# A state-space scan with a low-rank mixer: seven output blocks turned to token order by VectorE instead of TensorE

## The chip, the cores and the metric

The kernel runs on one core of a Trainium2 chip. The metric is the device time of one execution in microseconds (us), lower is better. Three runs of the kernel before took 227.44, 227.70 and 227.95 us; the median is 227.7 us.

Five engines work side by side, each on its own queue of instructions and in the order of that queue: TensorE (PE in the profile; PEld is its weight load), VectorE (DVE), ScalarE (ACT), GpSimd (POOL) and SyncE (SP, which here does nothing but issue DMA transfers). They wait for one another by semaphores.

## The reference

Two stages. The first is a gated linear recurrence over 768 tokens for 4 batches and 8 heads (head width 32, state width 16), worked in chunks. The second takes the heads side by side as 256 channels `x` (4, 768, 256) and computes

```python
xt = x.transpose(0, 2, 1)
h = xt @ U @ V                       # low rank 32, over the tokens
u = x + h.transpose(0, 2, 1)
ch = np.maximum(u @ w_ch1, 0.0) @ w_ch2   # 256 -> 1024 -> 256
return (u + ch).astype(np.float32)   # (4, 768, 256): tokens are rows
```

All of it is fp32. The weights come as 64-bit floats, which the kernel reads as pairs of 32-bit words and turns into fp32 itself.

## The kernel before

**Layout.** Tokens are handled with channels on the partitions: `yT[b]` is a tile of 128 partitions by 2 halves of channels (n = 0, 1) by 768 tokens. The mixer works on blocks (b, j): batch b, tokens j\*384 to j\*384 + 383, so there are eight blocks, (0,0) to (3,1). A function `block(n, j)` (line 751) gives the 128 x 384 piece of half n.

**Order.** Nothing is scheduled by a planner. The lists of words in `PLANS` (lines 34 to 73) give the order in which the program issues its work, and each engine's queue keeps that order. A word is a letter with numbers. The ones needed below are:

- `p`: product of all tokens with U (line 728), its PSUM result copied by ScalarE to `pT` (line 732)
- `x`: product of `pT` with V (line 739) into four PSUM banks, two tagged "x" and two tagged "z"
- `a`: VectorE adds these four products to `yT` (line 748); this frees the banks
- `S`: the block is split into three fp32r parts "near" (ScalarE, line 769), "far" and "both" (VectorE, lines 756 and 761), as tile `u`
- `f`, `e`, `h`: first and second product with `w_ch1` on TensorE, and the third step, on VectorE, which makes "far" and "both" of the result
- `g` and `m`, `M`: the scan's score products on TensorE (line 528), which take all four "x" and "z" banks, and VectorE's masking of them (line 541)
- `i`, `n`, `j`: the scan's output products (lines 654 and 678). The first product of `j` waits for a VectorE instruction, usually the one-column copy `settled` (line 605), which in turn waits for the products of `i` or `n`
- `d`: the next piece of `down(j)` for a block

**down(j)** (line 849) is a generator: each `d` in the plan runs it to the next `yield`. A block of batches 1 to 3 takes 14 pieces, a block of batch 0 takes 6. The pieces are products with `w_ch2` (line 774); then `whole` (line 857) adds the result to `yT` on VectorE; and the last two pieces, one for each half n, put the block into token order:

- three TensorE transposes of 128 x 128 into a PSUM bank tagged "w" (line 901)
- one ScalarE copy of 128 x 384 from PSUM into the tile `o` (line 902)
- behind the second half, one DMA of the whole block, 384 rows of 1 KB (line 904)

The block (3,1) goes through `rows(j)` (line 819) and not through `down`; so `down` handles seven blocks and its branch for `last` is never entered. Seven blocks with two halves each give 14 places in the queues. They come in seven pairs, and the plan sets what stands around them:

```
PLANS[1] ... R6 d1.0 g4 m4 p0 d1.0 M4 | PLANS[2] x1 R1 n0 s0 a1.0        block (0,0)
PLANS[2] ... e1.0.7 h1.0.6 i0 d2.1 d2.1 j0 h1.0.7 g2 y0 s2 m2 M2 n1 i1 d1.0 S1.1 f1.1.0   block (0,1)
PLANS[3] ... t2 e1.1.6 e1.1.7 p0 d1.0 | PLANS[4] x1 h2.1.6 h2.1.7 d2.0 d2.1 a1.0          block (2,0)
```

The wrapper `Kept` (lines 159 to 175) remembers the last VectorE instruction for the loads that are to start no earlier. It makes line 170 the line of nearly every VectorE instruction in the profile, so those are told apart by their tiles.

## Time and profile before

| what | value |
|---|---|
| median of three runs | 227.7 us |
| span of the profiled execution, first to last instruction | 225.2 us |
| median less span (no view of the profile shows what lies there) | 2.5 us |
| TensorE busy | 217.0 us, 3016 products |
| VectorE busy | 157.3 us, 339 instructions |
| ScalarE busy | 120.8 us, 283 instructions |
| GpSimd busy | 6.2 us |
| line 901, transposes | 42, pairs of places from 74.7 to 212.2 us |
| line 902, copies | 14, 476 to 483 ns each |
| line 904, stores of 384 KB | 7, issued from 78.4 to 213.1 us, 372 to 388 ns of SyncE's queue each, 2.5 to 4.4 us to landing |
| granted TensorE clock | 1.000 over the span |

The profile is of one execution, so durations read from it are summed against its span of 225.2 us; the profile names no other time of its own execution. The median of the separate runs lies 2.5 us above that span. In the timeline each row has the start in us, the time in us that the instructions of the row cover, the engine, the line, the operation, the tiles (written <- read), the shape and the count; in brackets stands how long the engine had been idle before it and what it waited for. Products on TensorE are pipelined: one starts while the one before it is still draining, so the distance from one start to the next tells more than a duration does. The same holds to a smaller degree on VectorE.

### The profile page before, as it was taken

Reading aid. Unit: us, or ns where it says so; the run is one execution under the profiler, and the core shown is the slowest. Engines: PE = TensorE matmul, PEld = TensorE weight load, DVE = VectorE, ACT = ScalarE, POOL = GpSimd, SP = SyncE. Lnnn points to the kernel's source line nnn. Section 1 sums busy time; section 2 is a strip of 40 time slices with the busy share of each in tenths; the row PEclk is TensorE's granted clock in tenths of the full one; section 3 lists DMA queues with packets and bytes.
Section 4 is the critical chain, followed back from the end, with each engine's and each line's share of the span. In section 5 each row is a group of like instructions: output and inputs, shape, how many; then the busy total and the mean of one; then the engine's idle time right before and its main releaser. Section 6 shows DMA issues by size and latency. Waiting matters only on the chain.

```text
span 225.2 us, 6994 instructions
## 1 busy us (share of the span) xinstructions
PE 217.0 (96%) x3016; PEld 180.5 (80%) x3016; DVE 157.3 (70%) x339; ACT 120.8 (54%) x283; POOL 6.2 (3%) x22
## 2 busy tenths in 40 slices
PE   7978899999999999999999999999999999999994
PEld 5657676665666678768999998799998799999993
DVE  3388899897996767879538827978557925765641
ACT  2353765579875425754616615385356434934820
POOL 4022000000000000000000000000000000000000
PEclk9999999999999999999999999999999999999999
DMA  6889779981950023642006200200000100010022
GB/s 89 141 120 147 113 171 220 240 177 41 167 76 4 0 73 41 89 59 73 4 3 90 75 1 3 76 0 0 4 0 3 43 30 0 3 68 3 0 70 70
DMA packets 69294, 14.56 MB, mean 65 GB/s; under 512 B 63568, under 2 KB 67472, under 8 KB 69264
## 3 DMA queue, kind: packets, MB, share of 16 engines
q1 hardware_dynamic: 69264, 14.13, 31.9%
q8 instruction: 23, 0.38, 0.7%
q14 instruction: 7, 0.06, 0.1%
HBM read 10.98 MB, written 3.15 MB: 63 GB/s over the span
## 4 chain that ended last, share of the span: by engine, by line
PE 89%; SPq 5%; DVE 2%; DMA 2%; issue 1%
PE x L774 33%; PE z L774 31%; SPq L196 4%; PE y L678 4%; PE y L654 4%; PE w L728 3%; PE w L901 2%; PE w L699 2%; PE x L528 2%; DMA bc<-in_C_dram 2%; PE w L496 2%; PE w L563 2%; PE x L739 2%; PE z L528 1%; PE z L739 1%
## 5 line engine op out<-in xcount | busy, mean ns | idle before, releaser
L170 DVE SCALAR_TENSOR_TENSOR words<-words 128x768 fp32r<-128x768 f32 (+6 forms) x44 | 34.6, 804 | 2.1 <-ACT words L420 1.1
L774 PE MATMUL z<-u,w 128*128 128x384 f32 x144 | 33.0, 349 | 0.0
L774 PE MATMUL x<-u,w 128*128 128x384 f32 x144 | 32.7, 346 | 0.0
L779 ACT ACTIVATE x<-x 128x384 f32<-128x384 f32 (+1 forms) x31 | 14.6, 470 | 28.2 <-PE x L774 27.6
L774 PEld LDWEIGHTS z<-u,w 128*128 128x128 f32 x144 | 25.0, 188 | 1.4 <-ACT z L779 0.2
L774 PEld LDWEIGHTS x<-u,w 128*128 128x128 f32 x144 | 24.9, 188 | 1.0
L774 PE MATMUL x<-words,w 128*128 128x384 f32 x120 | 24.7, 340 | 0.2 <-DVE yT L170 0.2
L774 PE MATMUL z<-words,w 128*128 128x384 f32 x120 | 24.6, 336 | 0.0
L779 ACT ACTIVATE z<-z 128x384 f32<-128x384 f32 (+1 forms) x30 | 14.2, 473 | 14.7 <-PE z L774 14.1
L170 DVE SCALAR_TENSOR_TENSOR words<-x,words 128x384 fp32r<-128x384 f32 x24 | 13.3, 553 | 11.7 <-ACT words L808 11.7
L774 PEld LDWEIGHTS x<-words,w 128*128 128x128 f32 x120 | 20.8, 188 | 0.5 <-DVE yT L170 0.4
L774 PEld LDWEIGHTS z<-words,w 128*128 128x128 f32 x120 | 21.1, 188 | 0.0
L170 DVE TENSOR_TENSOR yT<-x,yT 128x384 f32<-128x384 f32 x15 | 8.3, 553 | 16.0 <-PE x L774 15.4
L170 DVE SCALAR_TENSOR_TENSOR words<-z,words 128x384 fp32r<-128x384 f32 x24 | 13.2, 551 | 5.0 <-ACT words L808 5.0
L808 ACT ACTIVATE words<-x 128x384 fp32r<-128x384 f32 x24 | 11.8, 492 | 6.5 <-PE x L774 6.5
L808 ACT ACTIVATE words<-z 128x384 fp32r<-128x384 f32 x24 | 11.8, 492 | 4.5 <-PE z L774 4.5
L170 DVE TENSOR_TENSOR yT<-z,yT 128x384 f32<-128x384 f32 x15 | 8.3, 552 | 8.3 <-PE z L774 8.3
L654 PEld LDWEIGHTS y<-T,Sm 32*64 32x64 f32 x352 | 8.6, 131 | 4.7 <-issue 1.4
L654 PE MATMUL y<-T,Sm 32*64 32x64 f32 x352 | 11.9, 238 | 0.5 <-DVE settled L170 0.5
L678 PEld LDWEIGHTS y<-M,x 64*32 64x32 f32 x768 | 8.7, 105 | 4.5 <-issue 2.7
L678 PE MATMUL y<-M,x 64*32 64x64 f32 x768 | 11.3, 224 | 1.0 <-issue 0.7
L170 DVE SCALAR_TENSOR_TENSOR S<-S,kept,w 128x64 f32<-128x64 f32 x40 | 11.2, 279 | 1.6
(139 smaller groups left out, 382.3 us busy)
## 6 DMA issues: line engine op xcount, KB each, us to landing
words<-in_moe_w_ch_dram SPq DMA_DIRECT2D x7, 512.0 KB, 5.4
x<-in_x_dram SPq DMA_DIRECT2D x24, 128.0 KB, 3.5
out_dram<-o SPq DMA_DIRECT2D x5, 384.0 KB, 2.5
bc<-in_B_dram SPq DMA_DIRECT2D x24, 64.0 KB, 3.5
bc<-in_C_dram SPq DMA_DIRECT2D x12, 128.0 KB, 3.1
out_dram<-words SPq DMA_DIRECT2D x2, 384.0 KB, 3.6
words<-in_moe_w_ch_dram SPq DMA_DIRECT2D x2, 256.0 KB, 3.7
out_dram<-o SPq DMA_DIRECT2D x3, 128.0 KB, 1.7
```

What stands on the lines that cost most here:

```text
L170: self.last = call(*args, **kwargs)
L196: op = nc.sync.dma_start(**kwargs)
L496: nc.tensor.transpose(out=tp[:, i, v], in_=s["BC"][:, i, c + v].rearrange("p h n -> p (h n)"), identity=ident)
L528: nc.tensor.matmul(out=g[r][cols, c], lhsT=s["T"][rows, 0, c, cols], rhs=s["Cm"][rows, :, :, ts(2 * c + p, Q)].rearrange("r v t i -> r v i ...
L563: nc.tensor.matmul(out=s["A"][p][ts(r, Q), v], lhsT=s["bd"][half, v, 2 * r:2 * r + 2].rearrange("p h n -> p (h n)"), rhs=x_sb[k][half, v, ...
L654: product = nc.tensor.matmul(out=y[p][ts(r % 2, H), r // 2, c], lhsT=own[ts(r, Q)], rhs=s["T"][ts(r, Q), 1, :, ts(2 * c + p, Q)].rearrange ...
L678: product = nc.tensor.matmul(out=y[p][ts(i, Q), n, c], lhsT=x_sb[k][half, c, h], rhs=s["M"][half, h // 2, c, h % 2], start=fresh(k, p, [i] ...
L728: nc.tensor.matmul(out=p[ts(q, Q)], lhsT=U_sb[:, c], rhs=ytok[b][:, c, ts(q // 2, P)], start=(c == 0), stop=(c == NC - 1), skip_group_chec ...
L739: nc.tensor.matmul(out=h[q][:, :HS], lhsT=pT[rows], rhs=V4[rows], start=True, stop=True, skip_group_check=True)
L774: nc.tensor.matmul(out=t, lhsT=lhsT, rhs=rhs, start=start, stop=True, skip_group_check=True)
L779: nc.scalar.activation(t, t, AF.Copy, scale=1.0 + EPS)
L808: nc.scalar.activation(gs[j, m // 2][0][:, m % 2], t, AF.Relu, scale=NEAR)
```

## The change

In every block but (3,1), that is wherever `down` gets to this point, each half n is turned by one VectorE instruction, a stream transpose of 128 x 384 that transposes each 32 x 32 square in its place, from `yT` straight into the output tile. The squares then hold 32 tokens on 32 partitions by 32 channels. Four DMAs store a half, one for each group g of 32 partitions; each moves 384 pieces of 32 channels, 128 bytes, to its rows in the output. A half no longer uses TensorE, a "w" bank or ScalarE. The number of stores grows from 7 to 56. The transpose is called on the engine itself, not through the wrapper `Kept`, so it doesn't change which instruction the loads wait for.

```diff
@@ def down(j)
             o = (mix.tile([P, 2 * WCOLS], FP32, tag="o", name="o") if b else raw.tile(
                 [P, 2 * WCOLS], FP32, tag="words", name="words", bufs=NWORDS))
+            turned = o[:, :NCB * HS].rearrange("p (n t) -> p n t", n=NCB)
             o = o[:, :HS // P * DM].rearrange("p (k n d) -> p k n d", k=HS // P, n=NCB)
             for n in range(NCB):
...
                 if last and n:
                     yield
                     return
+                if (b, j) != (NB - 1, NBL - 1):
+                    nc.vector.transpose(out=turned[:, n], in_=block(n, j))
+                    for g in range(P // Q):
+                        nc.sync.dma_start(
+                            out=out[b, ts(j, HS)].rearrange(
+                                "(k t) (n g c) -> n g t k c", t=Q, n=NCB, c=Q)[n, g],
+                            in_=turned[ts(g, Q), n].rearrange("p (k c) -> p k c", c=Q))
+                    yield
+                    continue
                 t = bank("w", HS // P, P)
                 for k in range(HS // P):
                     nc.tensor.transpose(out=t[:, k], in_=block(n, j)[:, ts(k, P)], identity=ident)
                 nc.scalar.copy(out=o[:, :, n], in_=t)
```

Here P is 128, Q is 32, HS is 384, NCB is 2, NB is 4 and NBL is 2.

## The prediction

> **What bounds the kernel now.** I read the page first: busy times, slices, chain.

> ```profile
> PE 217.0 (96%) x3016; PEld 180.5 (80%) x3016; DVE 157.3 (70%) x339; ACT 120.8 (54%) x283; POOL 6.2 (3%) x22
> ...
> PE   7978899999999999999999999999999999999994
> ...
> DVE  3388899897996767879538827978557925765641
> ...
> PE 89%; SPq 5%; DVE 2%; DMA 2%; issue 1%
> ```

> TensorE is the bound: busy in every slice, 89% of the chain. VectorE's 70% is uneven: some slices are full, others a quarter. So the price of more VectorE work depends on the place. Line 901 and what a 384-column VectorE instruction costs come from that line's own view and the groups by shape:

> ```profile
> L901 PE MATMUL w<-ident,yT x42: 270/272/329, 74.7 to 212.2; 128*128 128x128 f32 x42
> ```

> ```profile
> L170 DVE TENSOR_TENSOR yT<-x,yT 128x384 f32<-128x384 f32 x15 | 8.3, 553 | 16.0 <-PE x L774 15.4 <-PE z L739 0.4 <-PE x L739 0.2
> ...
> L170 DVE TENSOR_SCALAR words<-words 128x384 int32<-128x384 int32 x2 | 0.6, 353 | 0.0
> ```

> Three transposes move TensorE's last end by 0.33 us (212.11 to 212.44 in the chain), 0.11 each; the 0.27 is mostly pipeline. Between products of another shape a place takes up to 0.48. So 14 x 0.33 = **4.6 us** is the most that TensorE alone can give; the 0.15 us more at six places are filling, which the next product pays instead.

> **What a transpose costs VectorE.** No transpose is in the trace. The nearest row has the same size and type: 553 ns long (425 for 256 columns in the same view, so 1.0 ns a column), but such adds start 0.465 us apart (78.90, 79.36, 79.83, 80.29). Below it, 353 ns for one source at a higher rate, about 0.27 apart by the same overlap. Above it, two passes: the 128x768 rows, 958 ns. I take **T = 0.50 us** of queue: the nearest row plus 0.03, an estimate for the first 32 columns at 1.0 ns, before a square can be given out turned; 0.27 and 0.96 stay for the range. [...]

> VectorE gains 14 x 0.50 = 7.0 us of queue, ScalarE loses 14 x 0.48 = 6.7, neither of which is the sum. What counts is what stands behind each pair in VectorE's queue. I followed the timeline at the seven pairs. Signs are changes of the end time.

> **(0,0), +0.74.**

> ```profile
> 77.27 0.55 PE L901 MATMUL w<-ident,yT 128*128 128x128 f32 x3
> 77.41 0.27 ACT L732 COPY pT<-w 128x128 f32<-128x128 f32 x1 [0.78 <-PE w L728]
> 77.75 0.59 PE L739 MATMUL x<-V,pT 32*128 32x384 f32 x2
> 78.90 0.55 DVE L170 TENSOR_TENSOR yT<-x,yT 128x384 f32<-128x384 f32 x1
> 79.71 0.59 PE L774 MATMUL x<-words,o 128*128 128x384 f32 x1
> ```

> VectorE has no gap from 74.44 to the adds at 78.90, and both transposes come before them. The add frees bank "x" at 79.45; TensorE takes it at 79.71, 0.26 later. With 2T in front it is free 1.00 later: 1.00 - 0.26 = +0.74, whatever TensorE saved (its second set only filled the wait for the pT copy). VectorE's next idle time, 3.10 us before 85.87, ends the delay there.

> **(0,1), +0.77.**

> ```profile
> 100.04 0.55 DVE L170 SCALAR_TENSOR_TENSOR words<-x,words 128x384 fp32r<-128x384 f32 x1
> 100.23 0.88 PE L901 MATMUL w<-ident,yT 128*128 128x128 f32 x6
> 100.51 0.14 DVE L170 COPY settled<-slot 128x1 f32<-128x1 f32 x1
> ...
> 101.04 0.42 PE L654 MATMUL y<-T,Sm 32*64 32x64 f32 x10
> ```

> Both transposes fall between the first two VectorE rows, and `settled` releases j0 on TensorE. It ends at 101.65 instead of 100.65; j0 had 0.39 to spare, so +0.61 where six transposes stood. Then `settled`, the step h, four masks and the split follow with one gap of 0.07: the split's "far" part ends 0.93 later than 104.46, and f1.1.0, which wanted it at 104.62, waits to +0.77.

> **(1,0), -0.66.** At 119.14 the delay goes into 0.42 us that VectorE idles before 120.44, at 124.23 it hits only copies whose user comes 7 us later (L728 at 135.7). TensorE keeps 2 x 0.33.

> **(1,1), -0.10.** VectorE's transposes fit into its idle 1.14 us before 138.63 and 0.60 before 140.91. But TensorE gains little: the masks from 138.63 to 140.05 free the banks of the next score products, which start at 140.05 already, and the next masks, to 142.33, free those of x1, whose last bank starts at 142.38. The transposes filled these waits.

> **(2,0), +0.56.**

> ```profile
> 176.13 0.96 DVE L170 SCALAR_TENSOR_TENSOR words<-words 128x768 fp32r<-128x768 f32 x1
> ...
> 177.53 0.56 DVE L170 TENSOR_TENSOR yT<-x,yT 128x384 f32<-128x384 f32 x1 [0.44 <-PE z L739]
> ...
> 178.14 1.66 PE L774 MATMUL x<-words,w 128*128 128x384 f32 x8 [0.15 <-DVE yT L170]
> ```

> VectorE is full from 170.43 to 177.09, idles 0.44, then does the add for which TensorE waits, with no slack. Both transposes come before it: 1.00 - 0.44. The 0.48 us of line 901 at 176.11 only covered the pT copy.

> **(2,1), -0.22.** At 192.17 the 0.52 us idle before 192.23 hides it and TensorE gains 0.33. At 194.94 the transpose stands before two h steps and the split. "Far" ends at 199.69, for a product that wants it at 200.12: slack 0.43. It moves by -0.33 + 0.50 to 199.86, and TensorE, 0.66 early, waits for it, about 0.44.

> **(3,0), -0.60.** Idle 0.38 before 208.56, 0.41 before 210.99 and 1.16 before 212.71 hide both. TensorE gains 0.66; the last "far" (215.20, wanted at about 215.5) costs some 0.05 back.

> **SyncE and DMA.** 56 stores at 0.38 us of queue are 21 us instead of 2.7, spread over seven blocks; a block's eight take 3 us where SyncE idles for 10 and more. The loads behind them are used many us later, so nothing. Cover gone would mean a load 3 us late. A 128-byte packet took 13 ns in this trace (x loads, reads), a 1 KB packet 47: a block is 3072 x 13 / 16 = 2.5 us of sixteen engines, against 1.1. Writing such rows isn't in the trace. At the end the eight stores of (3,0) are out by about 214.5 and the last three start at 218.9: cover 4 us. [...]

> **Added waits.** A reused output tile waits for eight stores instead of one: a handful of semaphore waits of 17 to 51 ns (rows at lines 902 and 901) in front of a transpose, +0.1 in all at (2,0).

> **Sum:** 0.74 + 0.77 - 0.66 - 0.10 + 0.56 - 0.22 - 0.60 + 0.10 = +0.6. The span goes from 225.2 to 225.8; with the same 2.5 us around it **228.3 us**, +0.3%. What a measurement can tell from no change is about 0.2%, 0.46 us. The sum changes by 7 us for each us of T (twice at three pairs, once at (2,1)), so T from 0.465 to 0.60 gives +0.35 to +1.3: the likeliest case's own range is 227.9 to 229.0.

> **Rivals.**
> 1. *VectorE's delay is hidden and TensorE's time comes back* (not slower). For: the chain, 89% TensorE. Against: the three places above. It decides by T: below 0.41 the sum is negative. At T = 0.27 it is 0.28 + 0.31 - 0.66 - 0.10 + 0.10 - 0.45 - 0.60 = -1.1: 226.6. With all three waits gone it ends at 227.7 - 4.6 = 223.1.
> 2. *Two passes*, T = 0.96: (0,0) 1.66, (0,1) 1.69, (2,0) 1.48, (2,1) about +0.2, the idle times at (1,0) and (3,0) overrun, together -0.5: +4.4, so 232.1. Against: the row of equal columns and bytes is the near one, and nothing in the trace takes two passes for one.
> 3. *Small stores bind*: SyncE or the sixteen engines fall behind and the last stores come 1 to 3 us late, 229.3 to 231.3. It needs over 60 ns per written 128-byte packet (5.9 us x 16 / 1536).
> 4. *The change doesn't do what it says*: the condition holds in all seven blocks, so 42 transposes and 14 copies go; I give it nothing.

> **Chances.** Forecast (227.7 to 229.1) 0.55; rival 1 0.25, of which 0.07 below 226; rival 2 0.10; rival 3 0.10. The forecast's low end is within 0.2%, as is a part of rival 1: same 0.25, faster 0.15, slower 0.60. Range 226.5 to 230.5.

> **What would show it.** In the profile after: 14 VectorE transposes of 0.5 to 0.6 us; TensorE idle, for the first time after 30 us, before L774 near 80, before L654 near 101 and before L774 near 178.6, each released by VectorE; no such wait at (1,0) and (3,0). I am wrong if the transposes take 0.9 us, if those three waits are missing, or if the last store of (3,0) lands after 218.

## The result, and the profile after

The changed kernel takes 229.92 us (median of 13 runs, 228.85 to 231.14) against 228.01 us (13 runs, 227.29 to 229.26) for the kernel before: **1.0082 times the time, interval 1.0057 to 1.0106**, some 1.9 us slower. The forecast was +0.3%, 0.6 us. Here and below the medians are of all executions, while a ratio and its interval leave out those more than 1.5% above the fastest of the same kernel (three in run 4, two in run 10).

The page of the changed kernel: busy times, the granted clock in 40 slices (tenths of full speed), the chain by engine.

```profile
PE 216.5 (95%) x2974; PEld 179.0 (78%) x2974; DVE 163.8 (72%) x353; ACT 115.1 (50%) x269; POOL 6.2 (3%) x22
...
PEclk9985999999999999999999999999999999999999
...
PE 84%; DVE 8%; SPq 3%; issue 2%; DMA 1%; ACT 1%; DVEq 0%
```

42 TensorE products and 14 ScalarE copies are gone, and VectorE has 14 instructions more. ScalarE lost 5.7 us of busy time, VectorE gained 6.5. TensorE lost only 0.5, in a span that is 3 us longer. In the chain TensorE gives up 5 points and VectorE takes 6: the end now hangs on VectorE in places. The profiled span, 228.2 us, belongs to an execution of 229.92 us, so 1.7 us lie around a span, not the 2.5 that the forecast took. The profile of before came from an execution with a short start.

**Where the time came from.** I paired every TensorE product, other than the transposes, of a run with the same product of the profile before. How much later it starts is its shift. The table has the growth of the shift over the stretch in which each block is turned (boundaries, in the time of before: 73.9, 98.0, 112.0, 137.2, 172.0, 188.0, 207.0 and 221.6 us). "Start" is the shift that a run already has at 73.9 us, ahead of anything that the change touches. There the executions of one kernel differ too: the two profiles of the changed kernel by 0.7 us.

| run, us | start | (0,0) | (0,1) | (1,0) | (1,1) | (2,0) | (2,1) | (3,0) | sum after start |
|---|---|---|---|---|---|---|---|---|---|
| forecast | | +.74 | +.77 | −.66 | −.10 | +.56 | −.22 | −.60 | +.5, and .1 for waits |
| changed kernel | 1.0 | +.86 | +.81 | −.39 | +.69 | +.40 | −.15 | −.19 | +2.0 |
| changed, again | 1.7 | +.81 | +.81 | −.39 | +.34 | +.41 | −.16 | −.19 | +1.6 |
| one store a block | .9 | +.86 | +.81 | −.39 | +.03 | +.40 | −.14 | −.19 | +1.4 |
| VectorE turn alone | 2.1 | +.86 | +.96 | −.03 | +.03 | +.40 | +.19 | +.01 | +2.4 |
| no turn | .9 | −.11 | +1.41 | −.39 | +.02 | −.03 | −.52 | +.05 | +.4 |
| no turn, again | .8 | −.11 | −.11 | −.38 | −.04 | −.04 | −.53 | −.18 | −1.4 |
| turn behind the add | 2.1 | +.74 | +.47 | +.69 | +.34 | −.03 | +.62 | −.18 | +2.7 |
| turn placed | .9 | +.13 | +.35 | +.68 | +.21 | −.03 | +.63 | −.19 | +1.8 |
| small stores alone | .9 | −.04 | +.01 | −.04 | −.04 | .00 | .00 | +.01 | −.1 |
| turn where nobody waits | 1.1 | −.05 | +.01 | −.38 | −.05 | −.03 | −.52 | −.18 | −1.2 |
| the same, with (0,1) | 1.3 | −.05 | +2.13 | −.37 | +.78 | −.02 | −.53 | −.19 | +1.7 |
| code pages moved | 9.7 | +.86 | +2.13 | −.39 | +.04 | +.41 | −.15 | +.07 | +3.0 |
| wait filled | 1.0 | +.85 | +.80 | −.38 | +.01 | +.41 | −.14 | −.19 | +1.4 |

**The new instruction.** The view of the changed kernel's line 901 (engine, operation, tiles, count; shortest, middle and longest duration in ns; first and last start):

```profile
L901 DVE STREAM_TRANSPOSE o<-yT x10: 566/570/572, 122.1 to 213.8; 128x384 f32<-128x384 f32 x10
L901 DVE STREAM_TRANSPOSE words<-yT x4: 536/562/571, 77.3 to 102.9; 128x384 f32<-128x384 f32 x4
```

It is one pass: 570 ns beside the add's 553. Two back to back delay what stands behind them by 0.96 us, so T is 0.48; the forecast had 0.50.

**(0,0).** Two rows of before, the masks M of the "z" banks and the first products with V that take those banks:

```profile
76.91 0.74 DVE L170 TENSOR_TENSOR M<-z,causal 128x256 int32<-128x256 int32 x2
77.76 0.59 PE L739 MATMUL z<-V,pT 32*128 32x384 f32 x2
```

The timeline of the changed kernel:

```profile
78.40 0.56 DVE L901 STREAM_TRANSPOSE words<-yT 128x384 f32<-128x384 f32 x1
78.69 0.91 PE L739 MATMUL x<-V,pT 32*128 32x384 f32 x4 [0.39 <-ACT pT L732]
78.88 0.72 DVE L170 TENSOR_TENSOR M<-z,causal 128x256 int32<-128x256 int32 x2
79.32 1.24 PE L739 MATMUL z<-V,pT 32*128 32x384 f32 x4
...
80.83 0.55 DVE L170 TENSOR_TENSOR yT<-x,yT 128x384 f32<-128x384 f32 x1
```

The size is as forecast, the place is not. The second transpose stands before the masks M of the two "z" banks, and the products with V want those banks. They came 0.01 us behind those for the "x" banks before (77.75, 77.76), and come 0.63 behind them now (78.69, 79.32). The wait before line 774 that the forecast named does not appear, since the delay was paid two steps earlier. The 0.39 us before 78.69 is the wait for the pT copy, which the second set of transposes used to fill.

**(0,1).** Two transposes in one row, then `settled`, then the product that waits for it:

```profile
102.39 1.03 DVE L901 STREAM_TRANSPOSE words<-yT 128x384 f32<-128x384 f32 x2
103.34 0.11 DVE L170 COPY settled<-slot 128x1 f32<-128x1 f32 x1
...
103.51 0.41 PE L654 MATMUL y<-T,Sm 32*64 32x64 f32 x9 [1.32 <-DVE settled L170]
```

This is the wait that the forecast named, and the longest that the change makes.

**(2,0).** The transpose, the add behind it, and the product that wants its bank:

```profile
180.48 0.57 DVE L901 STREAM_TRANSPOSE o<-yT 128x384 f32<-128x384 f32 x1
180.97 0.52 DVE L170 TENSOR_TENSOR yT<-x,yT 128x384 f32<-128x384 f32 x1
...
181.55 1.14 PE L774 MATMUL x<-words,w 128*128 128x384 f32 x5 [1.02 <-DVE yT L170]
```

The wait is 0.15 before, 0.48 of transposes that covered another wait, and 0.4 of new delay.

**(1,1).** What happens here was not in the forecast. TensorE stands still twice for no semaphore ("issue"):

```profile
143.56 0.48 PE L654 MATMUL y<-T,Sm 32*64 32x64 f32 x10 [0.36 <-issue]
...
147.84 0.48 PE L654 MATMUL y<-T,Sm 32*64 32x64 f32 x10 [0.41 <-issue]
```

Counting all of TensorE's instructions in the trace from the start (products, weight loads and its waits for semaphores), these stops stand at the numbers 4545 and 4801, which are 256 apart. Two like them are in the profile before, at 705 and 961 (20.50 and 24.86 us). 705 and 15 or 16 times 256 give 4545 and 4801, so all four lie on one grid of 256. The page has a queue for instructions of 16 KB a fetch (0.38 MB in 23).

The trace lists these fetches, as DMA packets with their times. The ones ahead of the four stops landed at 19.08, 23.48, 142.14 and 146.34 us, 1.4 to 1.5 us before TensorE went on. Taken in order, the first fetch goes with the instruction 449 of the grid, the second with 705, and so on. In all 14 profiles of this case none of the 308 instructions paired like this starts less than 1.20 us behind the landing of its fetch, and all but one of those with a distance of 0.3 us or more in front of them start 1.2 to 1.6 us behind it (the one is in a stretch where every pair of products is 0.32 us apart). By these times TensorE stood for its next 256 instructions, called a code page below. In the profile before, the same two counts fall at 140.18 and 144.31 us with no stop; by there the change has taken out at least 36 instructions, so other ones stand on the grid. The masks hide the first stop, the second reaches the end. The size differs from execution to execution: the gap in front of the second was 0.64 us here, 0.33 in the second profile and 0.04 with one store a block. At the first stop, in the eight profiles that have the same instruction there, it goes roughly with the time of the fetch: 0.14 and 0.22 us where the packet took 0.93 and 0.94, 0.35 where it took 1.06, 0.54 to 0.82 where it took 1.15 to 1.37. Two of these eight have no small stores at all (runs 4 and 5: 0.67 and 0.54), so the small stores are not needed for a stop.

### The profile page after: what moved, and what is told of

Same layout as the page of the kernel before. It is cut to its first block, busy times and chain, and to the rows that moved or that the text cites. A ratio compares the mean times of both kernels' runs of the same rounds, so it can differ in the third digit from the quotient of the medians.

```text
span 228.2 us, 6990 instructions
## 1 busy us (share of the span) xinstructions
PE 216.5 (95%) x2974; PEld 179.0 (78%) x2974; DVE 163.8 (72%) x353; ACT 115.1 (50%) x269; POOL 6.2 (3%) x22
## 4 chain that ended last, share of the span: by engine, by line
PE 84%; DVE 8%; SPq 3%; issue 2%; DMA 1%; ACT 1%; DVEq 0%
PE x L774 31%; PE z L774 29%; PE y L678 4%; PE y L654 4%; DVE words L170 4%; SPq L196 3%; PE x L528 2%; PE w L728 2%; PE w L563 2%; PE w L496 2%; PE z L528 2%; PE w L699 2%; PE z L739 1%; DMA words<-in_moe_U_dram 1%; PE x L739 1%
## 5 line engine op out<-in xcount | busy, mean ns | idle before, releaser
L170 DVE SCALAR_TENSOR_TENSOR words<-words 128x768 fp32r<-128x768 f32 (+6 forms) x44 | 34.6, 804 | 2.1 <-ACT words L420 0.9
L774 PE MATMUL x<-u,w 128*128 128x384 f32 x144 | 32.9, 346 | 0.2
L774 PE MATMUL z<-u,w 128*128 128x384 f32 x144 | 32.8, 349 | 0.0
L774 PEld LDWEIGHTS z<-u,w 128*128 128x128 f32 x144 | 25.0, 188 | 1.8 <-ACT z L779 0.6
L774 PEld LDWEIGHTS x<-u,w 128*128 128x128 f32 x144 | 25.0, 188 | 1.8 <-ACT x L779 0.6
L774 PE MATMUL x<-words,w 128*128 128x384 f32 x120 | 24.7, 340 | 1.0 <-DVE yT L170 1.0
L774 PE MATMUL z<-words,w 128*128 128x384 f32 x120 | 24.6, 336 | 0.0
L774 PEld LDWEIGHTS x<-words,w 128*128 128x128 f32 x120 | 20.8, 188 | 1.7 <-DVE yT L170 1.6
L774 PEld LDWEIGHTS z<-words,w 128*128 128x128 f32 x120 | 21.1, 188 | 0.0
L170 DVE SCALAR_TENSOR_TENSOR words<-x,words 128x384 fp32r<-128x384 f32 x24 | 13.1, 545 | 10.7 <-ACT words L808 10.7
L170 DVE TENSOR_TENSOR yT<-x,yT 128x384 f32<-128x384 f32 x15 | 8.2, 550 | 15.0 <-PE x L774 14.7
L170 DVE SCALAR_TENSOR_TENSOR words<-z,words 128x384 fp32r<-128x384 f32 x24 | 13.2, 550 | 4.3 <-ACT words L808 4.3
L654 PE MATMUL y<-T,Sm 32*64 32x64 f32 x352 | 12.9, 244 | 2.4 <-DVE settled L170 1.6
L654 PEld LDWEIGHTS y<-T,Sm 32*64 32x64 f32 x352 | 9.3, 136 | 7.1 <-issue 2.7
L170 DVE TENSOR_TENSOR yT<-z,yT 128x384 f32<-128x384 f32 x15 | 8.3, 550 | 8.3 <-PE z L774 8.3
L691 ACT COPY yT<-y 128x256 f32<-128x256 f32 x24 | 7.8, 384 | 10.4 <-PE y L654 10.4
L170 DVE SCALAR_TENSOR_TENSOR S<-S,kept,w 128x64 f32<-128x64 f32 x40 | 11.2, 280 | 2.2 <-issue 0.5
L528 PE MATMUL x<-Cm,T 32*64 32x128 f32 x192 | 11.9, 317 | 0.0
```

The source lines that it names most:

```text
L170: self.last = call(*args, **kwargs)
L528: nc.tensor.matmul(out=g[r][cols, c], lhsT=s["T"][rows, 0, c, cols], rhs=s["Cm"][rows, :, :, ts(2 * c + p, Q)].rearrange("r v t i -> r v i ...
L654: product = nc.tensor.matmul(out=y[p][ts(r % 2, H), r // 2, c], lhsT=own[ts(r, Q)], rhs=s["T"][ts(r, Q), 1, :, ts(2 * c + p, Q)].rearrange ...
L691: nc.scalar.copy(out=yp[:, :, :, p], in_=st[k]["y"][p])
L774: nc.tensor.matmul(out=t, lhsT=lhsT, rhs=rhs, start=start, stop=True, skip_group_check=True)
```

## The experiments

The theory after the result: (a) VectorE's delays cost what was forecast; (b) TensorE's gain was overrated; (c) the rest is page stops and noise of the start. The rivals: the stores, and the cost of the transposes wherever they stand.

**1. One store a block** (from the changed kernel).

```diff
-                    for g in range(P // Q):
+                    if n:
                         nc.sync.dma_start(
-                            out=out[b, ts(j, HS)].rearrange(...)[n, g],
-                            in_=turned[ts(g, Q), n].rearrange("p (k c) -> p k c", c=Q))
+                            out=out[b].rearrange("(j k p) m -> j p k m", j=NBL, p=P)[j],
+                            in_=o.rearrange("p k n d -> p k (n d)"))
```

> The changed kernel with its VectorE transposes, but each block stored by one DMA of 384 rows of 1 KB as before (so the values land in the wrong places of the output). Theory (VectorE's queue): the stores are off the path, so the time stays where the change put it, 1.3 to 2.0 us above the kernel before; the lower end if the 0.65 us that TensorE loses at the page of instructions near 147.8 us come from the fetch queuing behind small stores. Rival (small stores): all of the loss goes, within 0.4 us of the kernel before or faster.

229.62 us, 1.0082 [1.0055, 1.0109]: as slow as with 56 stores, though its profile has neither a stop at (1,1) nor a fall of the clock.

**2. Small stores alone** (from the kernel before).

```diff
-                if n:
+                for g in range(P // Q):
                     nc.sync.dma_start(
-                        out=out[b].rearrange("(j k p) m -> j p k m", j=NBL, p=P)[j],
-                        in_=o.rearrange("p k n d -> p k (n d)"))
+                        out=out[b].rearrange("(j k p) (n g c) -> j n g p k c", ...)[j, n, g],
+                        in_=o[:, :, n, ts(g, Q)])
```

> The kernel before, turned by TensorE and ScalarE, but each half stored by four DMAs of 384 pieces of 128 bytes. Theory (VectorE's queue): within 0.3 us of the kernel before. Rival (small stores): 1 to 2 us slower.

227.54 us, 0.9996 [0.9977, 1.0015]. With 1, the stores cost nothing that shows (within some 0.4 us). In the changed kernel the eight stores of (3,0) are out at 217.20 and the last three start at 221.97, a cover of 4.8 us. A store took SyncE's queue 0.47 us at the median, and all of them 29 us, where the forecast had 0.38 and 21.

**3. VectorE's turn alone**, into a tile that nobody reads (from the kernel before).

```diff
+    spare = const.tile([P, HS], FP32)
...
                 nc.scalar.copy(out=o[:, :, n], in_=t)
+                nc.vector.transpose(out=spare, in_=block(n, j))
```

> The kernel before with the fourteen VectorE transposes added into a spare tile that nobody reads; TensorE's transposes, ScalarE's copies and the stores stay. Theory (VectorE's queue): (0,0) +0.7, (0,1) +0.8, (2,0) +0.5, the other four blocks within 0.1 each: 1.7 to 2.2 us slower in all. Rival (small stores): no change, within 0.3 us.

230.60 us, 1.0119 [1.0089, 1.0150]. VectorE's side of the change by itself costs at least as much as the change: 2.7 us by the ratio, more than the 1.7 to 2.2 expected. The shifts, +.86, +.96, +.40 and +.19, stand at the four places where the forecast had VectorE last; the expectation had the fourth, (2,1), within 0.1.

**4. No turn**: the store reads `yT` as it is (from the kernel before; line 901's transposes, line 902's copies and their tiles are left out).

```diff
-                t = bank("w", HS // P, P)
-                for k in range(HS // P):
-                    nc.tensor.transpose(out=t[:, k], in_=block(n, j)[:, ts(k, P)], identity=ident)
-                nc.scalar.copy(out=o[:, :, n], in_=t)
...
-                        out=out[b].rearrange("(j k p) m -> j p k m", j=NBL, p=P)[j],
-                        in_=o.rearrange("p k n d -> p k (n d)"))
+                        out=out[b, ts(j, HS)].rearrange("t m -> (t m)").rearrange(
+                            "(p n t) -> p n t", p=P, n=NCB),
+                        in_=uT[:, :, ts(j, HS)])
```

> The kernel before without any turning in the seven blocks: no transposes, no copies, the block goes out as it lies in one DMA of rows of 1.5 KB (so the values land in the wrong places). It prices TensorE's share alone. Theory: TensorE's transposes mostly filled waits that end at other engines, so 0.8 to 2.0 us faster. Rival (TensorE's time comes back in full): 4.6 us faster.

228.54 us, 1.0021 [0.9996, 1.0046]: a miss. The experiment made a wait of its own at (0,1). The copy that refills `yT` now waits 2.61 us for the store, and TensorE for the copy:

```profile
104.27 0.96 PE L678 MATMUL y<-M,x 64*32 64x64 f32 x53 [1.14 <-ACT yT L691]
```

**5. No turn, again**, with the stores reading a tile that never changes.

```diff
-                        in_=uT[:, :, ts(j, HS)])
+                        in_=V4[:, None, :].to_broadcast([P, NCB, HS]))
```

> The kernel before without any turning in the seven blocks, as in the run without turning before, but the stores read a constant tile and not yT, so that no ScalarE copy into the next yT has to wait for a store (the output holds no result in these blocks). It prices TensorE's share alone once more. Theory: that wait of 1.14 us goes, so 0.6 to 1.6 us faster than the kernel before. Rival (TensorE's time comes back in full): 4.6 us faster.

226.88 us, 0.9936 [0.9912, 0.9959]. Without any transposes the kernel gains 1.4 us, of 4.6 that TensorE's 14 sets would be worth end to end. Part (b) holds. As nothing is turned here, hardly any way of turning can gain more in the present order.

**6. Turn right behind the add**, where VectorE mostly idles next (from the changed kernel). The new function `turn_out(n)` holds the transpose and the four stores of a half; the old place keeps only its `yield`.

```diff
                         whole(n, t)
+                        if not (n and (False)):
+                            turn_out(n)
```

> The changed kernel, each VectorE transpose and its stores moved forward to right behind the add that completes its half, so that TensorE's plan stays and only the place in VectorE's queue differs. Theory (VectorE's queue decides): each first half fits into the idle time before the second half's add (0.77 us or more in every block), the second halves at (2,0), (2,1), (3,0), (1,0), (1,1) fit into idle time too, and only (0,0) and (0,1) keep one transpose in front of a wait, some +0.2 us each: within 0.6 us of the kernel before, 1.5 to 2.4 us faster than the changed kernel. Rival (the work itself, wherever it stands, costs: stores, code pages, VectorE's load): stays 1.3 us or more above the kernel before.

231.08 us, 1.0105 [1.0075, 1.0136]: no better than the changed kernel (the intervals overlap), where 1.5 to 2.4 us less were expected. The theory behind it, that idle time of VectorE is slack, falls. The new shifts at (1,0) and (2,1), +.69 and +.62, stand where a step for which TensorE waits comes soon behind the gap. At (1,0) the chain runs from VectorE's `S` over ScalarE's `Sm` to its copy of bank x (this run's timeline):

```profile
122.83 0.69 ACT L595 ACTIVATE Sm<-S,slot 128x128 f32<-128x128 f32 x2 [3.15 <-DVE S L170]
...
123.43 0.47 ACT L779 ACTIVATE x<-x 128x384 f32<-128x384 f32 x1
...
123.95 0.61 PE L774 MATMUL x<-u,w 128*128 128x384 f32 x2 [0.63 <-ACT x L779]
```

**7. The same, with batch 0's second halves later.**

```diff
-                        if not (n and (False)):
+                        if not (n and (b == 0)):
                             turn_out(n)
...  PLANS
-  ... g4 m4 p0 d1.0 M4 | ... a1.0 a1.1 d2.1 S1.0 f1.0.0 ... i0 d2.1 d2.1 j0
+  ... g4 m4 p0 M4 | ... a1.0 a1.1 d2.1 S1.0 d2.0 f1.0.0 ... i0 d2.1 j0 d2.1
```

> As the run before it, but in batch 0 the second half is turned later: for (0,0) behind the next block's adds and split, for (0,1) behind the settled copy that releases j0. Theory (VectorE's queue): no transpose is left in front of a wait but the one at (0,1), so 0.2 to 0.4 us faster than the run before it, and 0 to 1.0 us faster than the kernel before. Rival: no better than the run before it.

230.28 us, 1.0077 [1.0050, 1.0103]. (0,0) and (0,1) fall to +.13 and +.35, which is what the move was for; (1,0) and (2,1) keep the new waits of 6. The expectation against the kernel before, 0 to 1.0 us faster, fails: it is 1.8 us slower. The intervals of 6 and 7 overlap, so that 7 is faster than 6 is shown by these two columns and not by the time.

**8. The changed kernel again**, no edit.

> The changed kernel once more, for a second profile. Theory (the idle 0.41 us of TensorE near 147.8 us are a page of instructions that falls on a dense stretch, since 84 instructions are gone): the same idle time, at the same instruction. Rival (chance of the DMA queues): it is not there. Time as the change's, 1.3 to 2.5 us above the kernel before.

230.18 us, 1.0079 [1.0053, 1.0105]. Every column repeats to 0.05 us, except the start and (1,1), where the stop stands at the same instructions with half the size.

**9. Turn where nobody waits.** VectorE has three long gaps, 3.1, 5.5 and 2.3 us, each behind the split S of a block, with nothing behind them that TensorE wants soon. The halves of (0,0), (2,0) and (2,1) go there; (0,1), which has no such place, is turned by TensorE as before (from the changed kernel).

```diff
  PLANS
-  R6 d1.0 g4 m4 p0 d1.0 M4 | ... a1.0 a1.1 d2.1 S1.0 f1.0.0
+  R6 g4 m4 p0 M4 | ... a1.0 a1.1 d2.1 S1.0 d2.0 d2.0 f1.0.0
-  e1.1.7 p0 d1.0 | x1 h2.1.6 h2.1.7 d2.0 d2.1 a1.0 a1.1 d2.1 S1.0 d2.1
+  e1.1.7 p0 | x1 h2.1.6 h2.1.7 d2.1 a1.0 a1.1 d2.1 S1.0 d2.0 d2.0 d2.1
-  f1.0.5 d2.1 h1.0.2 ... h1.0.5 d2.1 e1.0.7 ... S1.1 d1.0
+  f1.0.5 h1.0.2 ... h1.0.5 e1.0.7 ... S1.1 d2.1 d2.1 d1.0
...
-                if (b, j) != (NB - 1, NBL - 1):
+                if (b, j) not in ((0, 1), (NB - 1, NBL - 1)):
```

> The changed kernel with the two halves of (0,0), of (2,0) and of (2,1) turned later, behind the split of the next block (S1.0, S1.0, S1.1), after which VectorE idles for 3.1, 5.5 and 2.3 us before it next waits for TensorE; block (0,1) is turned by TensorE and ScalarE as before; (1,0), (1,1) and (3,0) as changed. Theory (a transpose costs only where TensorE waits on VectorE behind it): by the shifts measured so far -0.1 at (0,0), 0 at (0,1), -0.4 at (1,0), 0 to +0.4 at (1,1), 0 at (2,0), -0.5 at (2,1), -0.2 at (3,0): 0.8 to 1.2 us faster than the kernel before. Rival (VectorE's work costs wherever it stands): slower than before by 0.5 us or more.

226.60 us, 0.9942 [0.9919, 0.9965]: faster than both kernels, 1.3 us below the one before. Each column equals that of 5, no turn, to 0.12 us: the twelve transposes are free. The pair of (2,0), in its new place, and the wait that it used to lengthen, now down from 1.02 to 0.63 us:

```profile
178.69 1.66 PE L774 MATMUL x<-words,w 128*128 128x384 f32 x8 [0.63 <-DVE yT L170]
...
181.94 1.03 DVE L901 STREAM_TRANSPOSE o<-yT 128x384 f32<-128x384 f32 x2
```

**10. The same, with (0,1) by VectorE** at the changed kernel's place.

```diff
-                if (b, j) not in ((0, 1), (NB - 1, NBL - 1)):
+                if (b, j) != (NB - 1, NBL - 1):
```

> As the run before it, but (0,1) is turned by VectorE at the changed kernel's place. Theory: +0.8 us against the run before it, all of it between 98 and 112 us, so 0 to 0.4 us faster than the kernel before. Rival: no difference to the run before it.

229.24 us, 1.0036 [1.0004, 1.0068], with runs from 227.16 to 231.25. One pair costs 2.1 us by the ratios of 9 and 10, where its delay explains 0.8. The profile has two more costs. (1,1) has its page stops back (+.78). And 1.55 us behind the end of the 1.32-us wait, at 104.40 us, the granted clock falls. Busy time by stretch (us and count for each engine, then the granted clock, DMA share and GB/s):

```profile
100.00:104.40 4.40, 3.08 (x98) 2.17 (x98) 3.57 (x8) 1.54 (x5) 0.00 (x0) 1.00 0.18 28
104.40:107.80 3.40, 3.40 (x90) 3.11 (x77) 3.37 (x9) 0.41 (x1) 0.00 (x0) 0.50 0.42 63
107.80:111.00 3.20, 3.20 (x32) 2.87 (x31) 0.95 (x5) 1.36 (x3) 0.00 (x0) 1.00 0.17 25
```

Half the clock for 3.41 us: the column (0,1) reads 2.13, 1.32 more than in the profiles with the same wait and no fall.

**11. Code pages moved**: 20 small products at the start shift every later instruction (from the changed kernel).

```diff
+    pad = bank("x", P)
+    for _ in range(20):
+        nc.tensor.matmul(out=pad[:, :4], lhsT=ident, rhs=ident[:, :4], start=True, stop=True)
```

> The changed kernel with twenty small products more on TensorE in the first microseconds, where it waits for loads; nothing reads them. They move the places at which TensorE's instruction pages end by 40 instructions or more. Theory (the stall near (1,1) is a page end on a dense stretch): the shift at (1,1) is within 0.05 us of none, where the changed kernel showed 0.68 and 0.35 in two profiles; time 0 to 0.5 us below the changed kernel. Rival (the small stores hold up the fetch): the shift stays above 0.3 us.

239.13 us, 1.0501 [1.0446, 1.0556]: a miss as a timing, since the 20 products took 8.5 us and disturbed the start. Its profile still tells something: the stop at (1,1) is gone (+.04), and its longest stop, 1.65 us at 36.11 us, stands at the number 1217, on the same grid. The clock fell here too, to 0.50 for 3.41 us from 113.7, behind the same wait:

```profile
113.70:117.10 3.40, 3.40 (x90) 3.11 (x77) 3.37 (x9) 0.40 (x1) 0.00 (x0) 0.50 0.48 74
```

**12. Wait filled**: at (0,1) TensorE makes the six old transposes as well, and nobody reads them (from the changed kernel).

```diff
+                if (b, j) == (0, 1):
+                    t = bank("w", HS // P, P)
+                    for k in range(HS // P):
+                        nc.tensor.transpose(out=t[:, k], in_=block(n, j)[:, ts(k, P)], identity=ident)
                 if (b, j) != (NB - 1, NBL - 1):
```

> The changed kernel, but at (0,1) the six TensorE transposes stay, into a bank that nobody reads, so that they fill 0.8 us of the wait before j0. Theory (the wait of 1.32 us lets the granted clock fall to half for 3.41 us in some executions, 1.3 us each): the shift at (0,1) stays near +0.8 to +1.0 in the profile with no fall of the clock, the wait there is about 0.5 us, and the median is 0.2 to 0.7 us below the changed kernel's ratio of 1.008 to the kernel before, so 1.005 to 1.007, with runs closer together. Rival (the clock falls by chance, or seldom): the ratio stays at 1.008 or above.

229.09 us, 1.0043 [1.0024, 1.0063], runs from 228.45 to 229.70. Six products that do nothing take some 0.8 us off the changed kernel's cost (the two intervals still overlap a little), and its spread goes from 2.3 to 1.25 us. The end of `j0` comes no earlier (+.80):

```profile
103.44 0.41 PE L654 MATMUL y<-T,Sm 32*64 32x64 f32 x9 [0.52 <-DVE settled L170]
```

TensorE merely idles 0.52 us instead of 1.32. The twelve instructions also move the code pages, and (1,1) has no stop (+.01). So the gain is that of the clock, of the pages, or of both. What each is worth at the median stays open.

## Why the prediction was right or wrong

**The time.** 1.0082 times the 227.7 us that the forecast started from is 229.6 us. That is slower, as forecast, and inside the whole range of 226.5 to 230.5, but above the range that the forecast gave its own case, to 229.0 or 229.1. The whole range reaches so high for the rivals "two passes" and "small stores", and both fall. So the direction and most of the delays were foreseen, and two thirds of the size were not.

**Right.** T was 0.48 (forecast 0.50). Four terms with VectorE's delay came out at +.86, +.81, +.40 and −.15, for +.74, +.77, +.56 and −.22: together 0.07 us off, and 0.03 below the forecast with the 0.10 for added waits counted. That the sum is so close is partly luck: single terms are off by 0.04 to 0.16 and offset one another. Run 3 shows that VectorE alone makes these delays. The four rivals fall: the delay is not hidden (runs 3 and 12), a transpose is one pass, the stores cost nothing that shows (1 and 2), and the 42 products and 14 copies did go. One of the forecast's signs of being wrong came true without harm: the last store of (3,0) landed at 218.53 us, after 218, but all of that part stands 3.0 us later, and the next store starts at 221.97.

**Wrong in place.** At (0,0) the forecast saw the add as the step that TensorE waits for. It was the mask before it: a transpose was moved past M4, and M4's banks had only about 0.1 us to spare (0.96 of delay, +.86 of shift). The forecast had 0.26 to spare at the add; that the two are close, and the size nearly right, is luck.

**Wrong in size: the gain at (1,0) and (3,0)**, −.39 and −.19 for −.66 and −.60. The step that failed is "TensorE keeps 2 x 0.33". Run 5, with no VectorE work at all, has the same −.38 and −.18, so VectorE is not the cause. The first set of (1,0) only stood in front of a product that takes a bank from ScalarE. The rows of the changed kernel:

```profile
122.22 0.47 ACT L779 ACTIVATE x<-x 128x384 f32<-128x384 f32 x1
...
122.74 0.62 PE L774 MATMUL x<-u,w 128*128 128x384 f32 x2
```

The product starts 0.05 us behind the end of ScalarE's copy. In run 5 TensorE, 0.33 early at 119.65, has lost nearly all of that again by 120.36 (times of before). At (3,0) run 5 wins 0.33 twice. It loses 0.14 of each (at 210.03 and 212.81 in the times of before) at products that likewise start right behind ScalarE's copy; the second of these in run 5:

```profile
211.24 0.47 ACT L779 ACTIVATE z<-z 128x384 f32<-128x384 f32 x1 [0.22 <-PE z L774]
...
211.77 0.62 PE L774 MATMUL z<-u,w 128*128 128x384 f32 x2
```

It loses another 0.2 by 215.6, most of it at 215.35 and 215.47, to VectorE's "far" part, which the forecast priced at 0.05. These two terms, (1,0) and (3,0), are 0.68 us of the miss.

**Wrong in size: (1,1)**, +.03 to +.69 for −.10. That the transposes only filled waits there is right (run 5: −.04). The page stops, at 143.56 and 147.84 us here, are what the forecast had no term for. They were not at these instructions in the profile before, with at least 36 instructions more ahead of them, nor in run 12, with twelve more (+.01).

**Missing: the clock.** The forecast priced a wait of TensorE at its length. Here the 1.32 us of waiting at (0,1) were followed by 3.41 us at a clock of 0.50, another 1.3 us, in two of five profiles (runs 10 and 11).

Summed: 0.6 from the forecast, less 0.03, plus 0.27, 0.41 and 0.13 for the three terms, is the +1.4 of the runs without a stop (1 and 12). The stop adds 0.3 to 0.7 where it strikes, and the fallen clock 1.3 in some executions. The measured 1.9 lies between. But the median of run 1 is 1.9 too, and its one profile has neither, so how the last 0.5 us split stays open. Two slips in the forecast's own figures are small: at (2,1) its numbers make TensorE wait 0.40 us, not 0.44, and +0.35 from 227.7 is 228.05, not 227.9.

## What to carry to other kernels

Work moved to an engine with idle time was free here only where nothing behind that idle time was wanted soon (run 6: 1.0105). Look for the gaps behind which nobody waits, and put the work there (run 9: 0.9942), or leave that piece where it was. Instructions of the bound engine that stood in a wait were worth little when they were removed: 14 sets of transposes worth 4.6 us gave back 1.4 (run 5), since most filled waits for a copy or for a bank.
